# Attention with a gated MLP on one core: projections in groups of four tiles with two score blocks at their end, and another order of the first tiles and of the shift steps

## The chip, the core and the metric

The kernel runs on one core of a Trainium2 chip. The core has five engines that run side by side, each with its own queue in order: TensorE (PE, with its weight loads shown as PEld), VectorE (DVE), ScalarE (ACT), GpSimd (POOL) and SyncE (SP), which here issues all DMAs. The metric is the device time of one execution in microseconds (us).

## The reference

Layer norm feeds an attention block and an MLP; the MLP's output gates the attention's:

```
xn = layernorm(x)                               # x: 2048 x 512
q, k, v = split(xn @ wqkv)                      # 32 heads of 16
s = softmax(q @ k.T * 16**-0.5) @ v, heads joined, @ wo
h = relu(xn @ w1 + b1)**2                       # 512 -> 1792
out = x + s * silu(h @ w2 + b2)
```

All tensors are float32.

## The kernel before, in words

**Precision.** A product is made of three matmuls: both operands are split into a high and a low part (`split`, L78, on POOL, or with the high part on ACT; `split_psum`, L87, on ACT and DVE), and high x high, high x low and low x high are summed (`terms3`, L267). Softmax needs the row maximum of each score row before the exponential. Scores are therefore computed twice: once with query rows on the partitions for a maximum over 512 keys (`max_mm`, L293: one matmul of 512 columns and one DVE reduce, L313), and once with keys on the partitions for the exponential (`exp_mm`, L1270: one matmul and one ACT exponential, L1289). The maximum enters the second product as two extra rows of the query operand, a high and a low part.

**Units and blocks.** The work of attention is 32 units (4 heads by 512 queries), each of 64 maxima and of 16 blocks (128 keys): a block is four scores, four exponentials and the PV product (`pv_step`, L1293). The 512 blocks are numbered by `st`.

**Row halves.** Most matmuls contract over 64 rows, so PE takes two at a time, one in each half of its rows. The code calls the halves lanes. A lone matmul in one half leaves the other idle. A tile that is accumulated by both halves has its second half's first matmul wait for a DVE reduce that was issued behind the first half's last one.

**Start** (L1134 to L1197). `x` is loaded in 16 tiles of 128 tokens, with the four slices of V's weights between the first four. POOL splits these slices one after the other. The loop over `i` interleaves, for neighbouring tiles, statistics (`ln_stats`), normalisation (`ln_norm`), transposes by PE with ACT's copy (`ln_high`), the low part by DVE (`ln_low`), and 8 matmuls a step of projection tiles at full height (`pump`, L1111; `q_tile`, L988). There are 48 projection tiles (16 of V, 32 of Q and K) of 12 such matmuls; 16 are done here. Then the second weight load, the rings for K and Q and the loads of the first K heads and Q unit follow (L1178 to L1188). SP is not under a written order here: a scheduler places its DMAs.

**Lead** (L1202 to L1263). 31 tiles are made in row halves (`lead_halves`, L1032): 12 matmuls in the low half, then 12 in the high half, and the high half runs 23 steps late (`far`, `LAG`), beside the low half of the next tile. Each tile takes 5 maxima along. Banks rotate over three pools (`q_bank`, L980). At the end the high half's rest is flushed with one maximum for three steps. A finished tile is copied by ACT, split by POOL and stored by SP (`q_end`, L997). `b` counts tiles; loads, ring fills and stores are hung on its values.

**Main loop** (L1467). Blocks 0 and 1 carry 6 full-height matmuls each of the last tile (`slot` with `fill=6`); that tile is split into a tile of its own and its store is put off by 6 blocks (`later(6, ...)`, L1012). Blocks 2 and 3 have no extra work; from 4 on the MLP is fed in: for the first 256 tokens by `halves`, one block a slot, then by `long_slots` (L1365), four blocks each. In a long slot, two blocks run as one half with 12 dense matmuls in one lane and maxima and scores in the other. Ordinarily these take 8 maxima in two visits with a PV product behind each; here called an eight. If enough maxima are in hand (`ahead_m`, L1353, less a reserve that falls with `st`, or more freely beside a pending shift, `hosts`, L1360), they take 7 in one visit and both PV products together: a seven. The last 60 blocks carry the output projection (`wo_part`, L737), in wide slots once no maximum is left (`m_free`, L734).

**Shift** (`shift`, L336). When a unit's 64 maxima are done, `max_end` notes it (`late`), and two blocks later DVE reduces them (L338), forms the high and low part with two `scalar_tensor_tensor` steps (L340, L343), and transposes them (L347); SP stores the result (`keep`, L350) and loads it as rows of the query operand (`back`, L370). `later(n, fn)` puts a function off by n blocks, and `begin` (L1455) runs what is due.

PE's order is written out throughout; those of ACT, DVE and POOL in the start, the lead and the loop; SP's in the loop alone.

Of the kernel before, what the change touches and what calls it, by code (L numbers as in the profile page):

```python
# [16 lines left out]
P = 128  # L17
# [15 lines left out]
LAG = 8  # L33
# [3 lines left out]
EPS = 1e-5  # L37


@with_exitstack  # L40
def kernel(
# [31 lines left out]
    zero = const.tile([P, 16], F32, name="zero")  # L73
    nc.vector.memset(zero, 0.0)
# [23 lines left out]
    with ExitStack() as ph:  # L98
# [87 lines left out]
        def later(n, fn):  # L186
            waiting.append((now[0] + n, fn))
# [144 lines left out]
        def shift_due():  # L332
            if late and late[0][0] <= now[0]:
                shift(late.pop(0)[1])

        def shift(u):  # L336
            m4 = sp.tile([P, 16], F32, name="m4")
            nc.vector.tensor_reduce(m4, mxs[u], axis=AX.X, op=ALU.max)  # L338
            sh = sp.tile([P, 2, 16], F32R, name="sh")
            nc.vector.scalar_tensor_tensor(  # L340
                sh[:, 0], m4, -1.0, zero, op0=ALU.mult, op1=ALU.add
            )
            nc.vector.scalar_tensor_tensor(  # L343
                sh[:, 1], m4, -1.0, sh[:, 0].bitcast(F32), op0=ALU.mult, op1=ALU.subtract
            )
            sq = sp.tile([P, 32], F32, name="sq")
            nc.vector.transpose(sq, sh.rearrange("p i c -> p (i c)").bitcast(F32))  # L347
# [9 lines left out]
            if in_loop:  # L357
                later(1, keep)
                later(max(2, 16 * u - 9 - now[0]), back)
            else:  # L360
                keep()
                if u < 2:
                    back()
                else:
                    waiting.append((16 * u - 9, back))
# [371 lines left out]
        def wo_part():  # L737
            for k in range(15):
# [31 lines left out]
                def post():  # L770
# [9 lines left out]
                    nc.vector.tensor_tensor(g, ps[0], g, op=ALU.mult)  # L780
# [197 lines left out]
        lead = [0, 0, 0]  # L978

        def q_bank():  # L980
            lead[2] += lead[0]
            if lead[2] % 5 == 1:
                return pd.tile([P, 512], F32, name="pd_t")
            if lead[2] % 5 == 2:
                return pv.tile([P, 512], F32, name="po")
            return pe.tile([P, 512], F32, name="se")

        def q_tile(kind, m, c, last=False):  # L988
            ps = pd.tile([P, 512], F32, name="pd_t") if last else q_bank()
# [4 lines left out]
            q_end(kind, m, c, ps, last)  # L994
            yield

        def q_end(kind, m, c, ps, last=False):  # L997
            if kind == "v":
# [6 lines left out]
                return  # L1005
            if last:

                hl = pools["n"].tile([P, 2, 512], F32R, name="hl")
                raw = sp.tile([P, 512], F32, name="ot", bufs=1)
                nc.scalar.activation(raw, ps, AF.Copy)  # L1010
                split((hl[:, 0], hl[:, 1]), raw)
                later(6, lambda: qk_store(m, c, hl))  # L1012
                return
# [18 lines left out]
        def lead_halves(kind, m, c):  # L1032
            ps = q_bank()
# [3 lines left out]
            def emit(mm, lane, follow):  # L1037
# [4 lines left out]
                    start=first_ and lane == 0, stop=last_ and lane == 1,  # L1042
# [10 lines left out]
                if lane and last_:  # L1053
                    q_end(kind, m, c, ps)

            def behind(inst):
# [3 lines left out]
                [lambda mm=mm, lane=lane: emit(mm, lane, lane and mm is mms[0]) for mm in mms]  # L1060
                for lane in range(2)
            ], behind
# [81 lines left out]
        for ko in range(KO):  # L1144
            split((wa_t[:, 0, ko, 2 * P :], wa_t[:, 1, ko, 2 * P :]), raw_v[:, ko])
        for i in range(NT + 3):
            if i == 1:
# [3 lines left out]
            if 0 < i - 1 < NT:  # L1151
                ln_norm(i - 1)
            if 0 <= i - 3 < NT:
                ln_low(i - 3)
            if 0 <= i - 2 < NT:
# [10 lines left out]
            if i >= 3:  # L1166
# [5 lines left out]
                pump(8 if i > 3 else 6)  # L1172
# [8 lines left out]
        for n in range(8):  # L1181
            load_k(0, n)
# [344 lines left out]
```

## Time and profile before

| What | Value |
|---|---|
| median of 3 runs | 1639.32 us (1638.95 to 1640.37) |
| the profiled execution | 1642.99 us, span 1641.1 us |
| mean granted PE clock | 0.996 |
| PE busy | 1621.3 us (99%) |
| DVE busy | 1350.6 us (82%) |
| ACT busy | 1181.7 us (72%) |
| POOL busy | 516.4 us (31%) |
| HBM read, written | 144.84 MB, 53.99 MB |

The span runs from the first to the last instruction. Rows of the trace in order of time give start, duration, engine, source line, operation, output <- inputs, shape and count; a bracket behind them gives the idle time of the engine before it and what ended it. Rows of groups give busy time and the mean of one behind the bar. A PE row's duration holds the way through the array, so that neighbouring matmuls overlap; the distance between starts is what one costs. A table of stretches gives the length, each engine's busy time with its instructions, the granted clock (1.00 is full), the share of the DMA engines and GB/s. In the lists of waits stand the total, the number and the longest.

### The profile page before, as it was taken

How to read it: one execution, taken by the hardware profiler on the slowest of the kernel's cores; microseconds unless marked ns; L12 is line 12 of the kernel's file. 1: busy time of each engine (PE TensorE's matmuls, PEld its weight loads, DVE VectorE, ACT ScalarE, POOL GpSimd, SP SyncE). 2: the span in 40 equal slices, each digit the busy share in tenths (PEclk: the TensorE clock that was granted, in tenths of full speed). 3: DMA queues.
4: the chain of work that ended last, by engine and by line, in shares of the span. 5: the costliest groups of instructions: out<-in, count | busy, mean ns of one | idle time of the engine just before them, and what ended most of it. 6: DMA issues, size and time to landing. Idle time of an engine off the chain costs nothing.

```text
span 1641.1 us, 35386 instructions
## 1 busy us (share of the span) xinstructions
PE 1621.3 (99%) x13627; PEld 979.2 (60%) x13627; DVE 1350.6 (82%) x2335; ACT 1181.7 (72%) x2339; POOL 516.4 (31%) x541
## 2 busy tenths in 40 slices
PE   7999999999999999999999999999999999999998
PEld 6799666556656655565566556645665565454455
DVE  6399988887788888888888888888888888888843
ACT  6221477778878877787777777877877777777785
POOL 5335567513211321222123103311331133213224
PEclk9899999999999999999999999999999999999999
DMA  8596555426232522342333423343341442415444
GB/s 304 158 270 222 180 177 163 130 54 170 86 87 83 162 72 81 102 128 70 93 99 111 114 71 111 95 107 82 112 121 50 105 142 62 105 48 171 122 147 143
DMA packets 150465, 201.44 MB, mean 123 GB/s; under 512 B 50008, under 2 KB 67416, under 8 KB 148760
## 3 DMA queue, kind: packets, MB, share of 16 engines
q1 hardware_dynamic: 150296, 199.17, 41.6%
q8 instruction: 108, 1.77, 0.5%
q14 instruction: 61, 0.50, 0.1%
HBM read 144.84 MB, written 53.99 MB: 121 GB/s over the span
## 4 chain that ended last, share of the span: by engine, by line
PE 94%; DVE 2%; issue 2%; DMA 1%; POOL 0%; SPq 0%; ACT 0%; DVEq 0%
PE po L379 30%; PE pm_t L305 17%; PE pd_t L239 17%; PE se L1283 15%; PE pd_t L207 5%; PE se L1040 3%; PE pd_t L787 2%; DVE mx L313 2%; PE pd_t L1040 1%; PE po L1040 1%; PE se L991 1%; DMA ka<-k_d 1%; PE pm_t L1283 0%; DMA xt<-in_A_x_dram 0%; POOL wr_t L944 0%
## 5 line engine op out<-in xcount | busy, mean ns | idle before, releaser
L313 DVE TENSOR_REDUCE mx<-pm_t 128x1 f32<-128x512 f32 x2048 | 1267.9, 683 | 208.7 <-PE pm_t L305 123.1
L1289 ACT ACTIVATE pt<-se 128x512 f32<-128x512 f32 x1738 | 924.0, 615 | 227.3 <-PE se L1283 156.5
L305 PE MATMUL pm_t<-ka,qm 64*128 64x512 f32 x2048 | 784.5, 418 | 4.2 <-DVE mx L313 2.4
L1283 PE MATMUL se<-qe,ka 64*128 64x512 f32 x2009 | 735.0, 413 | 0.4 <-DMA qe<-sh_d 0.2
L379 PE MATMUL po<-pt,v 128*32 128x512 f32 x3554 | 526.6, 602 | 0.0
L305 PEld LDWEIGHTS pm_t<-ka,qm 64*128 64x128 f32 x2048 | 360.6, 185 | 219.5 <-DVE mx L313 205.2
L1283 PEld LDWEIGHTS se<-qe,ka 64*128 64x128 f32 x2009 | 350.5, 184 | 103.1 <-ACT pt L1289 61.8
L239 PEld LDWEIGHTS pd_t<-xc,w1s 64*128 64x128 f32 x2352 | 295.7, 187 | 47.3 <-issue 45.3
L239 PE MATMUL pd_t<-xc,w1s 64*128 64x256 f32 x2352 | 322.0, 286 | 0.0
L239 PE MATMUL pd_t<-w2t,hT 64*128 64x512 f32 x936 | 253.2, 406 | 0.0
L379 PE MATMUL po<-ex,v 128*32 128x512 f32 x542 | 226.5, 602 | 0.0
L1289 ACT ACTIVATE ex<-se 128x512 f32<-128x512 f32 x271 | 163.4, 616 | 42.1 <-PE se L1283 30.2
L239 PEld LDWEIGHTS pd_t<-w2t,hT 64*128 64x128 f32 x936 | 159.5, 184 | 48.5 <-issue 40.2
L379 PEld LDWEIGHTS po<-pt,v 128*32 128x32 f32 x3554 | 88.2, 108 | 154.3 <-issue 141.1
L558 POOL TENSOR_TENSOR r<-r 128x512 f32<-128x512 f32 x49 | 50.9, 1039 | 331.9 <-ACT r L555 331.9
L577 POOL TENSOR_TENSOR u<-u,b_t 128x512 f32<-128x512 f32 x16 | 20.7, 1296 | 365.0 <-ACT u L576 365.0
L207 PE MATMUL pd_t<-w2t,hT 64*128 64x512 f32 x408 | 106.1, 392 | 0.0
L207 PEld LDWEIGHTS pd_t<-w2t,hT 64*128 64x128 f32 x408 | 72.5, 184 | 9.6 <-DVE mx L313 0.7
L787 PE MATMUL pd_t<-wot,oc 64*128 64x512 f32 x267 | 76.9, 406 | 0.0
L417 POOL TENSOR_TENSOR ot<-ot,hl 128x512 f32<-128x512 f32 x31 | 39.8, 1284 | 109.1 <-DMA hl<-r_d 80.9
L83 POOL TENSOR_TENSOR hT<-r,hT 128x512 fp32r<-128x512 f32 x56 | 72.2, 1289 | 4.7
L1040 PE MATMUL se<-xT,wr_t 64*128 64x512 f32 x336 | 71.4, 390 | 0.0
(133 smaller groups left out, 1213.4 us busy)
## 6 DMA issues: line engine op xcount, KB each, us to landing
w1s<-w_d SPq DMA_DIRECT2D x196, 256.0 KB
k_d<-hl SPq DMA_DIRECT2D x32, 256.0 KB
xn_d<-xT SPq DMA_DIRECT2D x8, 1024.0 KB
q_d<-hl SPq DMA_DIRECT2D x16, 512.0 KB
qm<-q_d SPq DMA_DIRECT2D x128, 64.0 KB
qe<-q_d SPq DMA_DIRECT2D x128, 64.0 KB
ka<-k_d SPq DMA_DIRECT2D x32, 256.0 KB
hl<-r_d SPq DMA_DIRECT2D x31, 256.0 KB
```

Source lines behind the costliest of these rows:

```text
L83: (lo or nc.gpsimd).tensor_tensor(dst[1], raw, dst[0].bitcast(F32), op=ALU.subtract)
L207: mm = nc.tensor.matmul(out_, lh(r), rh(r), start=first_ and lane == 0, stop=last_ and lane == 1, skip_group_check=True,)
L239: mm = nc.tensor.matmul(out_, lh(r), rh(r), start=first_ and lane == 0, stop=last_ and lane == 1, skip_group_check=True,)
L305: nc.tensor.matmul(ps, qms[u][p][64 * j : 64 * j + 64, qb * P : (qb + 1) * P], kas[qd, p][64 * j : 64 * j + 64, kc * 512 : (kc + 1) * 512] ...
L313: return nc.vector.tensor_reduce(mxs[u][:, c, kc : kc + 1], ps, axis=AX.X, op=ALU.max)
L379: nc.tensor.matmul(po[32 * j : 32 * j + 32, :], vs[qd][:, (4 * kb + j) * VW : (4 * kb + j) * VW + 32], pts[j], start=(kb == 0), stop=(kb = ...
L417: nc.gpsimd.tensor_tensor(ot, ot, hl[:, 1].bitcast(F32), op=ALU.mult)
L558: nc.gpsimd.tensor_tensor(r, r, r, op=ALU.mult)
L787: inst = nc.tensor.matmul(ps[lane], oc[r, a, n, ts_], wot[r, b, n], start=m == 0 and (lane == 0 or wide), stop=m == kos and (lane == 1 or ...
L1040: inst = nc.tensor.matmul(out_, lh(r), rh(r), start=first_ and lane == 0, stop=last_ and lane == 1, skip_group_check=True,)
L1283: nc.tensor.matmul(se, kas[qd, j // 2][b : b + 64, kb * P : (kb + 1) * P], qes[u][j // 2][b : b + 64, :], start=True, stop=True,)
L1289: return nc.scalar.activation(pts[j], se, AF.Exp, scale=0.25)
```

## The change

- **Lead.** All 32 remaining tiles run in 8 groups of four (`lead_group`). Lane 0 does the first half of tiles 0 and 2 and the second half of 1 and 3; lane 1 the reverse. Both lanes begin and end a group together. `LEAD_AT` gives the places of 11 maxima in each lane (group 0 has none before its step 12). Banks are fixed: two of `pe`, one of `pd`, one of `pv`.
- **Scores.** In the last group the 8 scores and exponentials of blocks 0 and 1 are put in, after each twelfth of a lane, all of them in the third `pe` bank. The main loop begins with block 2, and the path of its own for the last tile is dropped.
- **SP** is in written order from the first K loads on; Q's pairs are loaded behind each four K loads, and some ring fills move.
- **Start.** V's slices 2 and 3 have their high parts made by ACT, and for x's first tiles the transposes come ahead of the next normalisation and statistics; the matmuls start one step earlier (3, then 9, then 8 a step) and 36 follow the loop instead of 48.
- **Shift.** Three `tensor_reduce` steps (maximum; negated maximum; negated sum of both as the low part) take the place of a reduce and two `scalar_tensor_tensor`. Store and load of the shift are run first among what is due, and before block 440 a shift may wait two blocks longer for a seven.
- **Sevens** come in couples (`seven`): one is taken only if two can be, and beside a pending shift a couple begins in the second half of a long slot.
- **Tail.** While maxima are left, an output tile is copied by ACT and multiplied by POOL instead of being multiplied by DVE; `wo_small` comes 8 blocks after its call instead of 3.

```diff
-        def later(n, fn):
-            waiting.append((now[0] + n, fn))
+        def later(n, fn, first=False):
+            waiting.insert(0 if first else len(waiting), (now[0] + n, fn))
...
-        def shift_due():
-            if late and late[0][0] <= now[0]:
+        def shift_due(slack=0):
+            if late and late[0][0] + slack <= now[0]:
...
-            m4 = sp.tile([P, 16], F32, name="m4")
-            nc.vector.tensor_reduce(m4, mxs[u], axis=AX.X, op=ALU.max)
-            sh = sp.tile([P, 2, 16], F32R, name="sh")
-            nc.vector.scalar_tensor_tensor(
-                sh[:, 0], m4, -1.0, zero, op0=ALU.mult, op1=ALU.add
-            )
-            nc.vector.scalar_tensor_tensor(
-                sh[:, 1], m4, -1.0, sh[:, 0].bitcast(F32), op0=ALU.mult, op1=ALU.subtract
-            )
+            sh = sp.tile([P, 3, 16], F32R, name="sh")
+            nc.vector.tensor_reduce(sh[:, 0].bitcast(F32), mxs[u], axis=AX.X, op=ALU.max)
+            nc.vector.tensor_reduce(sh[:, 1], mxs[u], axis=AX.X, op=ALU.max, negate=True)
...
+                nc.vector.tensor_reduce(
+                    sh[:, 2], sh[:, :2].bitcast(F32).rearrange("p i c -> p c i"),
+                    axis=AX.X, op=ALU.add, negate=True,
+                )
...
-                    nc.vector.tensor_tensor(g, ps[0], g, op=ALU.mult)
+                    else:
+                        h = ps[0]
+                        if not m_free():
+                            h = wos["f"].tile([P, D], F32, name="h", bufs=2)
+                            nc.scalar.activation(h, ps[0], AF.Copy)
+                    (nc.vector if wide or m_free() else nc.gpsimd).tensor_tensor(
+                        g, ps[0] if wide else h, g, op=ALU.mult
+                    )
...
-        for ko in range(KO):
-            split((wa_t[:, 0, ko, 2 * P :], wa_t[:, 1, ko, 2 * P :]), raw_v[:, ko])
+        for ko in range(2):
+            split_v(ko, False)
         for i in range(NT + 3):
+            if 2 <= i < 4:
+                if i == 3:
+                    split_v(3, True)
+                ln_high(i - 2)
+                ln_norm(i - 1)
+                if i == 2:
+                    split_v(2, True)
+                ln_low(i - 2)
+                rest.append(("v", i - 2, 0))
...
-        for n in range(8):
-            load_k(0, n)
-        qms[0] = load_q(0, "qm")
+        first.enter_context(tc.manual_schedule(engines={mybir.EngineType.SP}))
+        qms[0] = []
+        for p in range(2):
+            for n in range(4):
+                load_k(0, 4 * p + n)
+            load_q_pair(0, "qm", p, qms[0])
...
+        def lead_group(g):
+            items = [rest.pop(0) for _ in range(4)]
+            pools_ = [(pe, "se"), (pe, "se"), (pd, "pd_t"), (pv, "po")]
+            parts = [
+                lead_halves(*item, pool.tile([P, 512], F32, name=name), n % 2)
+                for n, (item, (pool, name)) in enumerate(zip(items, pools_))
+            ]
+            last = g == groups - 1
+            se = pe.tile([P, 512], F32, name="se") if last else None
+            streams = []
+            for lane in range(2):
+                own, other = parts[lane::2], parts[1 - lane :: 2]
+                mms = own[0][0] + own[1][0] + other[0][1] + other[1][1]
+                at = [i for i in LEAD_AT[lane] if g or i >= 12]
...
+                    if last and i % 12 == 5:
+                        kb, j = divmod(2 * (i // 12) + lane, 4)
+                        ops.append(
+                            lambda kb=kb, j=j: exp_mm(kb, j, pts.setdefault(kb, {}), False, se)
+                        )
...
+            for pair in zip(*streams):
+                for op in pair:
+                    op()
...
+        def seven(st):
+            if couple[0]:
+                couple[0] = False
+                return True
+            kept = 0 if late and st % 4 == 2 else max(0, 450 - st) // 16 * 2
+            couple[0] = ahead_m(sum(done_m) + 14 - kept, st + 4)
+            return couple[0]
```

221 lines of the change are left out of this document (98 added, 123 removed).

## The prediction

> **What bounds the kernel now.** I read the page's busy shares and its chain of waits first, then the lead stage in a table of time stretches, then the order in time of single engines where the change cuts.
>
> ```profile
> PE 1621.3 (99%) x13627; PEld 979.2 (60%) x13627; DVE 1350.6 (82%) x2335; ACT 1181.7 (72%) x2339; POOL 516.4 (31%) x541
> ```
>
> ```profile
> PE 94%; DVE 2%; issue 2%; DMA 1%; POOL 0%; SPq 0%; ACT 0%; DVEq 0%
> ```
>
> PE is the chain nearly everywhere. So an edit pays where PE runs half filled, slow or waiting, and costs where it adds PE steps. Five stretches make up the time from the lead's first half-array matmul to block 2 (124.76 us):
>
> ```profile
> 64.48:69.40 4.92, 4.00 (x17) 2.90 (x17) 1.98 (x3) 2.08 (x3) 4.17 (x3) 0.86 0.96 183
> 69.40:78.30 8.90, 8.90 (x36) 6.67 (x36) 6.35 (x10) 0.00 (x0) 0.00 (x0) 0.50 0.42 161
> 78.30:175.93 97.63, 97.50 (x837) 91.58 (x834) 90.33 (x151) 19.04 (x33) 46.64 (x51) 1.00 0.71 232
> 175.93:183.33 7.40, 7.05 (x34) 4.04 (x32) 7.40 (x13) 0.92 (x2) 3.21 (x4) 1.00 0.54 167
> 183.33:189.24 5.91, 5.57 (x24) 3.20 (x24) 4.75 (x8) 3.50 (x7) 1.91 (x2) 1.00 0.25 92
> ```
>
> Columns: stretch, length, busy PE, PEld, DVE, ACT, POOL (instructions), granted clock, DMA share, GB/s. Only the third row is full. In the first, one row half works alone (17 matmuls in 4.92 us); in the second the clock is 0.50; in the fourth only the late half's remainder is left and DVE sets the pace (7.40 of 7.40 busy); the fifth holds blocks 0 and 1 with the last tile at full height.
>
> **The sum is made against the profiled execution** (1642.99 us, span 1641.1, so 1.9 us lie around it). That is 3.67 above the median 1639.32 of the runs shown; I subtract the change from the median.
>
> **Lead in groups.** Stretches used here and below:
>
> ```profile
> 101.09:114.54 13.45, 13.45 (x119) 12.94 (x117) 12.51 (x21) 2.40 (x4) 6.19 (x7) 1.00 1.03 266
> 205.00:214.63 9.63, 9.23 (x87) 5.69 (x85) 8.81 (x16) 7.07 (x14) 6.64 (x10) 1.00 0.67 230
> 299.33:308.21 8.88, 8.88 (x68) 4.72 (x66) 8.07 (x16) 6.30 (x12) 4.65 (x5) 1.00 0.30 72
> 409.56:415.03 5.47, 5.47 (x59) 3.73 (x56) 4.28 (x8) 4.80 (x11) 1.04 (x1) 1.00 0.68 205
> 574.68:580.39 5.71, 5.71 (x59) 3.54 (x58) 4.97 (x9) 4.38 (x10) 0.91 (x1) 1.00 0.29 83
> 586.08:603.13 17.05, 17.02 (x143) 9.44 (x142) 14.31 (x27) 13.28 (x27) 2.95 (x3) 1.00 0.39 102
> 1576.05:1584.93 8.88, 8.88 (x74) 5.00 (x72) 1.38 (x2) 8.05 (x17) 2.57 (x2) 1.00 0.59 174
> ```
>
> The first row spans four lead tiles of 24 tile matmuls and 5 maxima: 116 matmuls, 58 pairs of row halves, 13.45/58 = 0.232 us a pair. After the change 32 tiles make 8 groups. A group has 96 tile matmuls and 22 maxima, 59 pairs, 13.68 us. Group 0 leaves out the maxima before step 12, and the shorter stream ends the pairing, so 96 + 16 = 56 pairs, 12.99. The last group adds 8 scores: 63 pairs, 14.61. Both halves start and end together, so rows one and four vanish. DVE keeps up: 12.51/21 = 0.596 us a maximum, 22 x 0.596 = 13.1 under 13.68, but only 0.6 is spare, so I allow 1.0 for the two shifts in the lead. The clock should stay whole, as the first maximum comes 12 steps (2.8 us) later and the K loads no longer stand on SP behind a weight load.
>
> The 8 scores all use one bank. A score's price:
>
> ```profile
> 183.36 0.47 PE L1283 MATMUL se<-qe,ka 64*128 64x512 f32 x1
> ```
>
> ```profile
> 183.01 0.60 ACT L1020 ACTIVATE raw<-pd_t 128x512 f32<-128x512 f32 x1 [3.45 <-PE pd_t L1040]
> 183.86 1.15 ACT L1289 ACTIVATE pt<-se 128x512 f32<-128x512 f32 x2 [0.25 <-DMA qm<-q_d]
> ```
>
> From the matmul's start to its exponential is 0.50, the exponential about 0.6: the bank is held 1.1 to 1.2 us. The halves' scores stand within one step of each other, so the second waits about 0.95 in PE's order, and everything behind it: 4 x 0.95 = 3.8 (bounds 1.9, if queued steps slip by, and 7.5, if all eight wait). The lead is then 12.99 + 6 x 13.68 + 1.0 + 14.61 + 3.8 = 114.5 against 124.76: **-10.3**. It does 170 maxima (before: 170, and 8 more in blocks 0 and 1).
>
> **Start.**
>
> ```profile
> 9.94 2.91 PE L991 MATMUL se<-wa_t,xT 128*128 128x512 f32 x6
> ...
> 13.35 2.12 PE L991 MATMUL se<-wa_t,xT 128*128 128x512 f32 x8
> ```
>
> Six matmuls take 2.91 where eight take 2.12: they wait for POOL, which splits V's four weight slices one after another. Now ACT makes two of the high parts and x's first transposes are copied ahead of the next normalisation. At the later rate the six cost 1.6, a gain of 1.3; **-1.3** (0, if ACT only takes the place of POOL, to -2.5, if the first tile also begins 1.2 earlier). The 16 full tiles ahead of the lead stay 16.
>
> **Hand-over to the MLP.** Before, the last tile's store was put off by 6 blocks; now the last two tiles end in the same step and SP runs in program order, so their stores stand ahead of the first w1 load.
>
> ```profile
> 183.70 0.62 POOL L82 TENSOR_SCALAR hl<-raw 128x512 fp32r<-128x512 f32 x1 [2.07 <-ACT raw L1020]
> 184.40 1.29 POOL L83 TENSOR_TENSOR hl<-raw,hl 128x512 fp32r<-128x512 f32 x1
> ...
> 192.41 0.41 POOL L82 TENSOR_SCALAR w1s<-ex 128x256 fp32r<-128x256 f32 x1 [0.40 <-DMA ex<-in_B_w_dram]
> 192.90 0.73 POOL L83 TENSOR_TENSOR w1s<-ex,w1s 128x256 fp32r<-128x256 f32 x1
> ```
>
> ```profile
> 189.34 0.39 SPq L451 DMA_DIRECT2D ex<-in_B_w_dram  x1
> ```
>
> ```profile
> 196.17 0.40 PE L207 MATMUL pd_t<-xc,w1s 64*128 64x256 f32 x2
> ```
>
> Copy 0.7, two splits of 1.95, stores 0.5: the load goes about 5.1 us after the lead's end. Load to split was 192.41 - 189.34 = 3.1, the first half's split 1.2: the MLP could begin at 9.4. Blocks 2 and 3 cover 196.17 - 189.24 = 6.9. PE waits 2.5, and 0.5 more for the second half: **+3.0** (0, if the loads aren't held, to 4.5, if POOL is a split behind).
>
> **Sevens.** A pair of blocks in a long slot does 8 maxima (5.71 in the fifth row above) or, with enough in hand, 7 (5.47 in the fourth). One is in hand for each maximum beyond 96 + 4 per block and the reserve; block 2 is now met with 170 instead of 178, so 8 sevens become eights: 8 x 0.22 = **+1.7** (1.5 to 2.0). The coupling moves some pairs of sevens. The sixth row holds an eight and an isolated couple that began in a first half: 17.05 - 5.71 = 11.34, where two sevens in a run take 10.94. By the planner's rule about four couples in the MLP's first product begin in a second half now: up to 4 x 0.4 gained, none if the entry costs there too; **-0.8** (+0.8 to -1.6). `first=True` and the later `wo_small` change the order of DMAs with blocks to spare: 0.
>
> **Shift steps.**
>
> ```profile
> L340 DVE SCALAR_TENSOR_TENSOR sh<-m,zero 128x16 fp32r<-128x16 f32 x30 | 7.7, 258 | 1.0
> ```
>
> ```profile
> L338 DVE TENSOR_REDUCE m<-mx 128x16 f32<-128x64 f32 x30 | 6.3, 210 | 0.0
> ```
>
> ```profile
> 207.65 0.96 DVE L340 SCALAR_TENSOR_TENSOR sh<-m,zero 128x16 fp32r<-128x16 f32 x1
> ```
>
> ```profile
> 1107.17 1.15 DVE L343 SCALAR_TENSOR_TENSOR sh<-m,sh 128x16 fp32r<-128x16 f32 x1
> ```
>
> ```profile
> 207.54 1.04 POOL L516 TENSOR_TENSOR r<-r 128x512 f32<-128x512 f32 x1 [3.12 <-ACT r L513]
> ```
>
> The two-input step at 207.65 started inside POOL's operation and ended with it (208.61 and 208.58). The one-input reduce has a mean of 210 ns over its 30, so it isn't held. The three blocks around the held step took 9.63 (second of the seven stretches), around one that ran freely 8.88 (third): 0.75 lost. DVE's order in time shows three such places outside a couple, the first and the last being the two rows above; in a couple the 16 PV matmuls hide them. The new steps, a negated reduce and a reduce over two rows of 16, each read one tensor; I price them as the 210 ns row and give back 0.8 a place: **-2.5** (0, if they are held as well, to -2.6; below that nothing, since no other place lies on PE's path). The Trainium skill's "VectorE: DVE Perf Modes", Rules for kernel authors, calls `tensor_reduce` on a hot path the slowest DVE operation and advises restructuring; taken at its word this term would be 0 or above and the sum -7.1. The row of 210 ns against 258 with waits speaks against it here.
>
> **Tail.** With 8 maxima left at block 486 the new test no longer refuses a seven; one maximum stays over, so the slot at 488 isn't run wide. It needs 2 x (14 x 0.232 + 1.9) = 10.3 instead of 8.88 (seventh row), the 1.9 from
>
> ```profile
> 412.61 1.92 PE L379 MATMUL po<-pt,v 128*32 128x512 f32 x16
> ```
>
> That is +1.4; the seven gives back 0.2, and two products of 0.68 leave DVE's queue of maxima,
>
> ```profile
> 1556.72 0.68 DVE L780 TENSOR_TENSOR g<-pd_t,g 128x512 f32<-128x512 f32 x1
> ```
>
> worth 0.6: **+0.6** (-0.8 to 1.4).
>
> Sum: -10.3 - 1.3 + 3.0 + 1.7 - 0.8 - 2.5 + 0.6 = -9.6; 1639.3 - 9.6 = **1629.7 us** (the profiled execution 1633.4).
>
> **Rivals.**
> *Covered hand-over and cheap bank*: the loads pass in time and half the bank waits are filled: -9.6 - 3.0 - 1.9 = -14.5, 1624.8. For it: POOL's first w1 split (192.41) stood 3.8 us ahead of the first MLP matmul (196.17), so there is cover that I may undercount. Against it: SP cannot pass a store that waits.
> *Clock falls at the hand-over*: the stretch with clock 0.50 followed pauses of under 2 us with half the array idle, and blocks 2 and 3 are thin too. Another such 8.90 us at half speed costs 4.45: -5.1, 1634.2. By the Trainium skill's "TensorE: Matmul & The Clock Gate", Part 1, the clock falls after an idle window of about 3.4 us, which this 3.0 us wait would not fill; by that rule the forecast stands.
> *DVE paces the groups*: the page's mean for a maximum is longer,
>
> ```profile
> L313 DVE TENSOR_REDUCE mx<-pm_t 128x1 f32<-128x512 f32 x2048 | 1267.9, 683 | 208.7 <-PE pm_t L305 123.1
> ```
>
> and 22 x 0.683 = 15.03, 1.35 over a group; six groups cost 8.1: -1.5, 1637.8. Against it: back to back DVE took 0.596.
> *Slower, SP in program order*: waits of SP in the stretch 40 to 190 us, longest first,
>
> ```profile
> SPq L964 <- POOL hl L83: 14.7, 7, 3.2
> SPq L1003 <- ACT vt L1000: 14.6, 4, 11.8
> SPq L967 <- POOL hl L83: 6.7, 8, 1.0
> SPq L967 <- POOL hl L82: 4.8, 5, 1.5
> SPq L370 <- DMA sh_d<-sq: 4.4, 2, 2.3
> ```
>
> are 45.2 us; if they all line up ahead of a unit's Q loads, which have 48 maxima (2.2 groups, 30 us) of slack, the maxima stop for 15 us and PE behind them: +5.4, 1644.7. It turns slower from a lateness of 13 us on.
>
> **Numbers.** About 0.2% (3.3 us) is what a measurement of this kernel can tell from no change: 1636.0 to 1642.6. Chances: forecast 0.56, covered 0.18, clock 0.11, DVE pace 0.10, SP 0.05. The first three are faster: 0.85; the fourth the same, 0.10; the last slower, 0.05. The range 1623.5 to 1637.0 takes in the first three with their terms' bounds and leaves out most of the other two.
>
> **What would show it.** The stretch from the first half-array matmul to block 2 should be about 114 us with clock 1.00 throughout; groups of 22 maxima 13.7 apart; four PE pauses of about 1 us in the last group; SP's w1 load about 5 us after the last tile and PE waiting 2 to 4 us before the MLP's first matmul; no shift step over 0.25 us; 66 runs of seven maxima before block 440, where DVE's order in time shows 74 today. It is wrong if groups take over 14.5, if the clock dips, or if the main loop from block 60 on is over 3 us longer.

## The result and the profile after

| | before | after |
|---|---|---|
| median of 4 runs each | 1639.84 us (1638.95 to 1640.44) | 1648.68 us (1646.99 to 1652.24) |
| the profiled execution | 1642.99, span 1641.1 | 1649.66, span 1647.8 |

The change makes the kernel slower, by half a per cent: ratio 1.0051, 95% interval 1.0037 to 1.0066. The forecast was 1629.7. In the page of after PE is busy 4.5 us less than before, yet the chain of waits is no longer PE alone:

```profile
PE 1616.8 (98%) x13639; PEld 966.1 (59%) x13639; DVE 1344.2 (82%) x2331; ACT 1183.9 (72%) x2343; POOL 515.7 (31%) x540
...
PE 91%; issue 2%; DMA 2%; POOL 1%; DVE 1%; SPq 1%; ACT 1%; DVEq 0%; POOLq 0%; ACTq 0%
```

So work was saved and time was lost to waits (half clock costs PE about 4.5 us in the trace of before and 5.4 in that of after). Where, is seen by five marks that both traces have: the first half-array matmul, the begin of block 2, the reciprocal at the end of the first unit and that at the end of the 30th, and the end of the span.

| stretch | before | after | difference | forecast |
|---|---|---|---|---|
| up to the first half-array matmul | 64.48 | 65.50 | +1.0 | -1.3 |
| lead, up to block 2 | 124.76 | 123.75 | -1.0 | -10.3 |
| block 2 to the first unit's end (hand-over) | 59.54 | 65.80 | +6.3 | +2.2 |
| to the 30th unit's end (loop) | 1312.12 | 1309.59 | -2.5 | -0.8 |
| to the end (tail) | 80.20 | 83.16 | +3.0 | +0.6 |

In the column of the forecast the shift steps' three places stand where the prediction has them, one in the hand-over and two in the loop. The rows of the marks, from DVE's order in time, before and after:

```profile
248.78 0.24 DVE L403 RECIPROCAL sm<-sm 128x16 f32<-128x16 f32 x1
...
1560.90 0.24 DVE L403 RECIPROCAL sm<-sm 128x16 f32<-128x16 f32 x1
```

```profile
255.05 0.24 DVE L403 RECIPROCAL sm<-sm 128x16 f32<-128x16 f32 x1
...
1564.64 0.24 DVE L403 RECIPROCAL sm<-sm 128x16 f32<-128x16 f32 x1
```

The lead of after in a table of stretches, cut at the begin of groups 0, 1, 5, 6 and 7, at block 2 and where the blocks run evenly again:

```profile
65.50:78.55 13.05, 13.05 (x113) 11.86 (x114) 9.33 (x15) 3.18 (x5) 6.82 (x4) 1.00 1.01 288
78.55:134.11 55.56, 55.56 (x474) 47.37 (x472) 54.64 (x92) 10.66 (x20) 23.53 (x27) 1.00 0.86 280
134.11:156.83 22.72, 16.06 (x122) 12.71 (x118) 14.02 (x23) 2.28 (x4) 9.50 (x11) 0.85 0.67 232
156.83:170.94 14.11, 14.11 (x121) 10.86 (x118) 13.97 (x26) 2.50 (x5) 7.83 (x9) 1.00 0.42 155
170.94:189.25 18.31, 16.22 (x129) 12.59 (x126) 14.14 (x24) 7.01 (x13) 8.40 (x9) 1.00 0.41 138
189.25:209.12 19.87, 14.89 (x92) 7.38 (x92) 11.53 (x18) 10.17 (x19) 11.44 (x19) 0.83 0.76 235
```

Group 0 takes 13.05, four full groups 55.56 (13.9 each), the last one 18.31. One group takes 22.72 and has PE busy for 16.06 of it. Without this stop of 8.8 us the lead would take 114.9, close to the forecast of 114.5. Inside the stop:

```profile
137.96:144.56 6.60, 0.00 (x0) 0.00 (x1) 1.03 (x2) 0.60 (x1) 2.48 (x4) 0.81 0.96 331
144.56:148.95 4.39, 4.39 (x20) 3.50 (x22) 1.50 (x3) 0.00 (x0) 3.15 (x3) 0.51 0.84 318
```

PE stands still for 6.60 us, and the next 20 matmuls run at a clock of 0.51; half of their 4.39 us, 2.2, makes up the rest of the 8.8. The list of waits from 134 to 150 us names the chain, to be read from PE upward, and SP's order in time shows what stood ahead of the stores:

```profile
ACT raw L1011 <- POOL hl L84: 11.4, 3, 7.9
DVE mx L314 <- PE pm_t L306: 8.5, 3, 7.3
POOL hl L83 <- DMA k_d<-hl: 7.1, 2, 6.5
PEld pd_t L1030 <- ACT raw L1011: 7.1, 1, 7.1
PE pd_t L1030 <- ACT raw L1011: 6.7, 1, 6.7
```

```profile
127.23 0.65 SPq L350 DMA_DIRECT2D sh_d<-sq  x1
132.54 2.08 SPq L370 DMA_DIRECT2D qe<-sh_d  x4
134.66 0.39 SPq L136 DMA_DIRECT2D ka<-k_d  x1
135.10 0.57 SPq L1271 DMA_DIRECT2D xn_d<-xT  x1
135.77 2.41 SPq L974 DMA_DIRECT2D k_d<-hl  x2
138.28 1.04 SPq L971 DMA_DIRECT2D q_d<-hl  x1
```

PE waits for a bank that ACT has not copied, ACT for a raw buffer, POOL for one of three split buffers (`hlp`), and that for a store. The store was issued at 135.8, behind SP's wait of 4.7 us (127.88 to 132.54) for the shift's own store. At the hand-over `xc` is loaded behind the stores of the last two tiles:

```profile
189.95 0.56 SPq L451 DMA_DIRECT2D ex<-in_B_w_dram  x1
190.61 1.49 SPq L974 DMA_DIRECT2D k_d<-hl  x2
193.73 0.53 SPq L971 DMA_DIRECT2D q_d<-hl  x1
194.31 2.65 SPq L493 DMA_DIRECT2D xc<-xn_d  x4
```

PE waits for it, and then half the clock is gone:

```profile
PE pd_t L208 <- DMA xc<-xn_d: 4.1, 2, 2.9
```

```profile
195.80:198.74 2.94, 0.00 (x0) 0.03 (x1) 0.69 (x1) 0.60 (x1) 0.74 (x2) 1.00 0.95 273
200.53:206.98 6.45, 6.45 (x33) 4.06 (x35) 2.39 (x4) 2.51 (x5) 3.46 (x7) 0.50 0.74 220
```

### The profile page after: what moved, and what is told of

Read it like the earlier page. It is cut to its first block, busy times and chain, and to the rows that moved or that the text cites. A ratio compares the mean times of both kernels' runs of the same rounds, so it can differ in the third digit from the quotient of the medians.

```text
span 1647.8 us, 35386 instructions
## 1 busy us (share of the span) xinstructions
PE 1616.8 (98%) x13639; PEld 966.1 (59%) x13639; DVE 1344.2 (82%) x2331; ACT 1183.9 (72%) x2343; POOL 515.7 (31%) x540
## 4 chain that ended last, share of the span: by engine, by line
PE 91%; issue 2%; DMA 2%; POOL 1%; DVE 1%; SPq 1%; ACT 1%; DVEq 0%; POOLq 0%; ACTq 0%
PE po L379 29%; PE pd_t L240 16%; PE pm_t L306 16%; PE se L1224 15%; PE pd_t L208 6%; PE se L990 2%; PE se L1030 2%; PE pd_t L794 1%; PE po L1030 1%; PE pd_t L1030 1%; DVE mx L314 1%; DMA sh_d<-sq 0%; PE pm_t L1086 0%; DMA hl<-r_d 0%; DMA xc<-xn_d 0%
## 5 line engine op out<-in xcount | busy, mean ns | idle before, releaser
L306 PE MATMUL pm_t<-ka,qm 64*128 64x512 f32 x2048 | 795.9, 417 | 0.9 <-DVE mx L314 0.6
L555 ACT ACTIVATE r<-pd_t,b_t 128x256 f32<-128x256 f32 x98 | 42.1, 496 | 32.7 <-PE pd_t L240 32.7
```

Source lines behind the costliest of these rows:

```text
L306: nc.tensor.matmul(ps, qms[u][p][64 * j : 64 * j + 64, qb * P : (qb + 1) * P], kas[qd, p][64 * j : 64 * j + 64, kc * 512 : (kc + 1) * 512] ...
L555: nc.scalar.activation(r[:, i], ps[:, i * CW : (i + 1) * CW], AF.Relu, bias=b1_t[:, fo : fo + 1])
```

## The experiments

All traces are compared with that of the changed kernel by the same marks. The table has one profiled execution of each (time, then the five stretches, in us):

| run | time | start | lead | hand-over | loop | tail |
|---|---|---|---|---|---|---|
| before | 1642.99 | 64.48 | 124.76 | 59.54 | 1312.12 | 80.20 |
| after | 1649.66 | 65.50 | 123.75 | 65.80 | 1309.59 | 83.16 |
| e1 | 1649.58 | 65.06 | 123.16 | 64.41 | 1309.56 | 85.61 |
| e2 | 1643.63 | 65.86 | 114.88 | 65.22 | 1309.64 | 86.20 |
| e3 | 1646.27 | 68.44 | 118.79 | 65.57 | 1309.43 | 82.17 |
| e4 | 1641.65 | 65.04 | 116.64 | 65.31 | 1309.44 | 83.37 |
| e5 | 1648.66 | 64.97 | 124.28 | 65.51 | 1309.62 | 82.52 |
| e6 | 1646.49 | 66.32 | 124.42 | 64.75 | 1309.38 | 79.83 |
| e7 | 1648.86 | 64.63 | 124.56 | 64.77 | 1309.93 | 83.11 |
| e8 | 1642.39 | 65.17 | 115.54 | 64.86 | 1309.52 | 85.51 |
| e9 | 1635.74 | 65.91 | 114.87 | 63.98 | 1309.47 | 79.77 |
| e10 | 1635.90 | 65.11 | 114.90 | 63.47 | 1310.91 | 79.71 |
| e11 | 1630.18 | 65.49 | 111.66 | 62.02 | 1309.54 | 79.69 |
| e12 | 1634.61 | 64.29 | 120.07 | 58.67 | 1309.52 | 80.25 |
| e13 | 1635.65 | 64.24 | 120.86 | 58.67 | 1309.85 | 80.28 |
| e14 | 1643.95 | 65.69 | 123.96 | 60.21 | 1309.57 | 82.77 |
| e15 | 1655.39 | 65.23 | 123.93 | 66.22 | 1315.01 | 83.21 |
| e16 | 1634.56 | 65.19 | 111.67 | 66.61 | 1309.53 | 79.70 |

Single executions differ, those of the kernel before by up to 8 us (below). The loop differs least: it takes 1309.4 to 1309.9 in the 13 kernels here that have the changed loop as it is or without its last seven.

**The stop: order, buffers or full DMA engines.** Four edits, one each:

```diff
 # e1_rows_later
-                    back()
+                    later(4, back)
 # e2_ring_five
-        hlp = right(qs, "hlp", 3)
+        hlp = right(qs, "hlp", 5)
 # e3_bias_early: the loads of b1_t and b2_t from k == 4 to ahead of
 # the first load_k
 # e4_sp_free
-        first.enter_context(tc.manual_schedule(engines={mybir.EngineType.SP}))
```

> The changed kernel, but in the lead the load of a unit's shift rows is issued four tiles after the store that it must wait for, instead of right behind it. In the changed kernel the seventh group of the lead takes 22.7 us where the others take 13.7 to 14.1: a stop of 8.8 us. Theory A, SP's written order: SP waits 4.6 us for the shift's store to land and issues the rows for 2.1 us, and the finished tiles' stores stand behind it, so the buffer of POOL's split comes free late. Then the stores at 135.8 go some 6.5 us earlier, the stop falls below 2 us, the clock stays whole there, and the time falls by 7 to 9 us to about 1640. Theory B, three buffers for two tiles that end together are too few: the stop stays over 4 us. Theory C, the DMA engines are full (busy share 1.0 from 110 to 120 us) and the stores land late whatever their order: the stop changes by less than 1.5 us.

> The changed kernel with five buffers instead of three for the split tiles of the lead. Two more buffers are half a group, 7 us, of slack for the stores. Theories A and B both let the stop of 8.8 us fall below 2 us (A: the stores are as late as before, 6.5 us, but nobody waits for them; B: no tile waits for a buffer any more); the time falls by 7 to 9 us. Theory C, full DMA engines: the lateness only moves to a later group, and the lead becomes shorter by less than 3 us.

> The changed kernel with the loads of the two bias vectors taken out of the lead (SP spends 3.5 and 2.7 us on issuing them at 115 us) and put ahead of the first loads of K. If SP's lateness is a sum (theory A in its wide form), 6.2 us less of it lets the stop of 8.8 us fall below 3 us. If only the shift's round trip counts (A in its narrow form) or the buffers alone (B), the stop stays over 6 us, because SP has caught up by 123 us in either case. Theory C, full DMA engines: 256 KB less in the full stretch, under 1 us. At the new place the loads may hold the first loads of K and cost up to 3 us ahead of the lead.

> The changed kernel with SP not under a written order in the lead: the scheduler places its DMAs, as in the kernel before. Theory A: the scheduler puts finished tiles' stores ahead of the wait for the shift, the stop falls by 5 us or more. Theory B: the stop stays over 4 us. At the hand-over the loads of the MLP's first data may also pass the last tiles' stores: of the 6.3 us that stretch cost, up to 3 us come back if so.

The group of the stop, in the four kernels in this order:

```profile
133.66:155.75 22.09, 16.36 (x120) 12.65 (x118) 14.01 (x22) 2.88 (x5) 11.95 (x14) 0.85 0.66 237
```

```profile
134.47:148.29 13.82, 13.82 (x121) 11.07 (x118) 13.66 (x22) 2.29 (x4) 7.57 (x9) 1.00 0.92 324
```

```profile
137.04:154.75 17.71, 15.67 (x120) 12.28 (x118) 13.98 (x22) 2.28 (x4) 8.26 (x10) 0.90 0.70 247
```

```profile
135.40:149.22 13.82, 13.82 (x120) 11.06 (x118) 13.66 (x22) 2.29 (x4) 7.58 (x9) 1.00 0.49 180
```

With the rows later the stop stays (22.09): the shift's round trip alone, my first theory, is refuted. In that kernel the stores were issued at 125.7 to 128.1, and POOL got its buffer only at 133.8. The DMA view from 120 to 130 us shows what the engines did meanwhile:

```profile
DMA  9999997799943310469699479997996988999999
GB/s 203 255 220 238 261 319 167 110 82 62 65 27 12 7 1 1 57 188 172 197 139 270 57 107 262 221 320 172 164 188 131 311 287 303 344 393 418 418 401 442
DMA packets 4234, 2.00 MB, mean 200 GB/s; under 512 B 3652, under 2 KB 3652, under 8 KB 4184
...
b_t<-in_B_b_dram SPq DMA_DIRECT2D x1, 7.0 KB
```

One load of 7 KB, `b1`, reads 1792 elements of 4 bytes that lie apart. The rate falls to 62 GB/s while the engines are 0.9 busy, and then with their share to 1 GB/s; the stores come behind what has queued up. The Trainium skill's "DMA: Bandwidth & Descriptors", Rules for kernel authors, says that a last dimension that isn't contiguous becomes one descriptor for each element; the 3652 packets under 512 B, about two for each element, agree. With the bias loads moved, the group falls to 17.71, though not to 13.8, and the lead begins 2.9 us later, at 68.44, behind the moved loads. Five buffers or SP's free order remove the stop wholly (1643.63 and 1641.65 in one run each). So there were two delays ahead of the stores. Taking both away, with three buffers left:

```diff
 # e8_rows_and_bias: e1, and
-                    nc.sync.dma_start(b2_t, b2[None, :].to_broadcast([P, D]))
...
+            if b == 24:
...
+                nc.sync.dma_start(b2_t, b2[None, :].to_broadcast([P, D]))
```

> The changed kernel with three buffers as it stands, but with both suspected causes of the stop taken away: the shift's rows are loaded four tiles after their store, and the two bias loads (one of them 7 KB in packets of 4 bytes) go to tile 24, past the full stretch. Taken alone, the rows left 8.2 us of the stop of 8.8 and the bias loads 3.8. Theory, a queue in order (SP's and the DMA engines') with three buffers as its slack: with both gone the stop falls below 1 us and the seventh group takes 13.7 to 14.5. Theory, three buffers are too few whatever the order: at least 3 us stay. At tile 24 the bias loads may make a stop of their own: then the eighth group is over 20 us instead of 18.3.

```profile
133.78:148.26 14.48, 14.08 (x120) 11.05 (x118) 13.95 (x22) 2.28 (x4) 8.25 (x10) 1.00 0.67 233
```

The stop is 0.6 us, and the last group took 18.32, so the bias loads at tile 24 hurt nobody. Shown: two things stand ahead of the stores, SP's wait and the bias loads. Each alone makes a stop (3.8 us with SP's wait left in e3, 8.2 with the bias loads left in e1), together 8.8, so both have to go; the slack is the number of split buffers, and five of them mend it as well. Not shown: which part of the bias loads does it, the small packets, the 256 KB of `b2` or the 6.4 us that SP spends on issuing both in e1; e3 and e8 move all of it together. The totals of e2 and e8 fall by less than the stop, because their tails are 3.0 and 2.4 us longer, at a clock of 0.91 from 1580 to 1600 us (1.00 in the changed kernel); e1's is too. What makes it fall there is open. SP's free order (e4) gives back only 0.5 at the hand-over, where up to 3 were thought possible.

**The hand-over.** The last two tiles' stores wait in the list of what is put off, in buffers of their own; for one of them two exponential tiles are borrowed:

```diff
+                if (m, c) == (3, 3):
+                    two = [free_pt.pop(), free_pt.pop()]
...
+                    waiting.append((6, store))
...
+                if (m, c) == (7, 3):
...
+                    waiting.append((7, lambda: qk_store(m, c, hl)))
 # e5_store_later gives the two tiles back in store, e14 at block 16:
+                    waiting.append((16, lambda: free_pt.extend(two)))
```

> The changed kernel, but the stores of the last two tiles of the lead are put off to blocks 6 and 7, as the kernel before did with its last tile; their split halves stand in buffers of their own. Theory, stores ahead of the MLP's loads: in the changed kernel PE waits 2.9 and 1.2 us for xc at 196 to 200 us and runs blocks 2 to 5 in part at a clock of 0.66. With xc issued at about 189.5 instead of 194.3, these waits fall below 1 us in sum, the clock stays whole, and 3 to 5 us of the 6.3 come back. Rival, POOL's queue: the four splits of the last tiles (7.8 us) end at 193.7 in either case and the split of w1 stands behind them; then less than 1.5 us come back and PE waits for w1 instead of xc.

> The changed kernel with the last two tiles' stores put off, with the borrowed buffers given back at block 16 instead of block 6. In the first try the fifth PV product of the main loop came 5.8 us earlier than in the changed kernel, before an exponential waited 3.35 us for a borrowed buffer. Theory, the hand-over is worth those 5.8 us: at the first unit's end 5 to 6.5 us less than the changed kernel, the clock whole from 190 to 220 us, the stop at 138 us unchanged. Rival, another wait at block 6 follows whatever the buffers: below 2 us.

The first try took the wait for `xc` away (0.5 us left) and gave it back at once: an exponential waited for the store of the tile that I had lent, and the clock fell behind it. The row of ACT in e5:

```profile
209.01 2.21 ACT L1246 ACTIVATE pt<-se 128x512 f32<-128x512 f32 x4 [3.35 <-DMA q_d<-pt]
```

With the tiles kept until block 16, PE is busy for 18.27 of the 20.00 us behind block 2 in e14, at full clock, and the first unit ends at 249.86 instead of 255.05, 5.2 us less, as expected; the stop of the lead was there as before (22.91).

```profile
190.00:210.00 20.00, 18.27 (x150) 9.75 (x151) 16.16 (x27) 14.21 (x29) 13.17 (x21) 1.00 0.81 257
```

**The tail.**

```diff
 # e6_no_late_seven
-            couple[0] = ahead_m(sum(done_m) + 14 - kept, st + 4)
+            couple[0] = st < 480 and ahead_m(sum(done_m) + 14 - kept, st + 4)
```

> The changed kernel without sevens from block 480 on; so no maximum stays over at block 488. Theory: the maximum left over costs twice, a thin slot in place of a wide one (10.9 instead of 8.9 us) and the last unit's shift about 10 us later, whose rows PE then waits for (1.2 us). Expected from block 480 on: PE's wait for the rows gone, one slot wide again, 2.5 to 3.5 us less; the output products moved to ACT and POOL keep a gain of up to 0.6 over the kernel before. Rival, the products on ACT and POOL cost the tail: less than 1 us comes back.

In after one maximum stays over, and with it the last unit's shift:

```profile
1578.22 0.69 DVE L314 TENSOR_REDUCE mx<-pm_t 128x1 f32<-128x512 f32 x1 [6.61 <-PE pm_t L306]
```

```profile
1593.30 0.47 PE L1224 MATMUL se<-qe,ka 64*128 64x512 f32 x1 [1.23 <-DMA qe<-sh_d]
```

In e6 the last three maxima run at 1571.10 and the shift at 1573.0 instead of 1581.8. From the end of the 30th unit to the end after needs 83.16, e6 79.83, before 80.20:

```profile
1564.64:1647.80 83.16, 76.01 (x564) 43.38 (x560) 26.18 (x48) 55.62 (x111) 29.29 (x24) 0.98 0.42 140
```

```profile
1564.87:1644.70 79.83, 73.93 (x564) 42.28 (x560) 26.96 (x49) 55.53 (x111) 30.64 (x25) 0.99 0.45 146
```

**The start.** e7 puts the start of the kernel before (the loop over `i` and V's slices) into the changed kernel.

> The changed kernel with the start of the kernel before (V's slices all on POOL, normalisation ahead of the transposes, 8 matmuls a step from the fourth step on, 48 behind the loop). Theory: in the changed start PE is a step ahead of the low part of x that DVE makes, and waits 2.4 us for it at 28 us behind a split that stands ahead on DVE; the gain of 1.1 us up to the second tile is lost there. So the first half-array matmul comes at 64.3 to 65.0 instead of 65.5. Rival, the later DMAs of the start (SP's stores, the rings) set the lead's begin: it stays at 65.5 or becomes later. Either way the stop at 138 us keeps its size, 7 to 10 us.

In after PE waits in the start for the low part of x:

```profile
30.88 1.90 PE L990 MATMUL se<-xT,wa_t 128*128 128x512 f32 x7 [2.42 <-DVE xT L1094]
```

In e7 this wait is 0.53, and the lead begins at 64.63. But the same start gives 64.97 to 66.32 in the other kernels here that share it, and 65.49 and 65.19 in e11 and e16 with the start of before. The wait is shown, the net loss of about 1 us is not settled.

**The shift steps.** e12 and e13 are one kernel: before with the three reduces alone. e15 is the changed kernel with the steps of before.

```diff
 # e12, e13: into before; e15: the same taken out of the changed kernel
-            nc.vector.scalar_tensor_tensor(
-                sh[:, 0], m4, -1.0, zero, op0=ALU.mult, op1=ALU.add
-            )
...
+            nc.vector.tensor_reduce(sh[:, 1], mxs[u], axis=AX.X, op=ALU.max, negate=True)
```

> The kernel before with the shift's three reduces alone. Theory, the two-input step is held by POOL: three places of 0.8 us each are gained, near 207, 1107 and 1570 us; no shift step is over 0.25 us; 1.6 to 2.6 us less than before. Rival, the held steps are covered: below 0.8.

> The kernel before with the three reduces alone, timed. Its trace gained 3.6 us at shift steps (four places) and 4.7 us in the lead, where the profiled execution of the kernel before had a stretch at half clock that this one lacks. Theory, that stretch belongs to single executions and not to the kernel: the median falls by the 3 to 4 us of the shift steps, to 1635.5 to 1637. Rival, the reduces bring the clock back as well: the median falls by 7 to 9 us, to 1631 to 1633.

> The changed kernel with the shift steps of the kernel before (a reduce and two steps with two inputs). Theory, the reduces save 0.8 to 0.9 us at each place where POOL works beside an uncovered shift: 2 to 4 us more than the changed kernel from block 2 on, in steps of 0.7 to 1.0, with held steps of 0.5 to 1.2 us on DVE. Rival, in the changed kernel's order the shifts fall beside other work: under 1 us.

Against the trace of before, e12 gains 0.87 ahead of the first unit's end, 0.90 between the first two, 0.95 at the 19th to 20th and 0.48 near the 29th, where e13 gains only 0.10; it is 3.4 in all (3.1 in e13), and no step took over 0.22. The expected places near 207 and 1107 us paid; the one near 1570 paid nothing (tail 80.20 before, 80.25 in e12), and the held step at 254.79 paid in its stead. Taking the reduces out of the changed kernel (e15) costs 5.8 us of span, 5.4 of it in the loop, more than the 2 to 4 expected; there 15 of the 60 two-input steps behind block 2 are over 0.25, where in before 6 are. Each of these 21 began inside an operation of POOL and ended at most 0.05 us after it. The mean of the first step nearly doubles (258 before):

```profile
L343 DVE SCALAR_TENSOR_TENSOR sh<-m,zero 128x16 fp32r<-128x16 f32 x32 | 15.3, 479 | 1.1
```

But e12's trace is 8.3 us shorter than that of before, not 3.4. The rest is in one place, the stretch that the prediction quotes with a clock of 0.50 and 36 matmuls. The same 8.90 us in e12:

```profile
69.40:78.30 8.90, 8.59 (x67) 6.97 (x68) 8.61 (x15) 0.60 (x1) 0.00 (x0) 1.00 0.45 164
```

Nearly twice the matmuls at full clock, with nothing changed there. Block 2 begins in e12 at

```profile
184.36 0.50 PE L1282 MATMUL se<-qe,ka 64*128 64x512 f32 x1
```

where before it began at 189.24. Timed, the reduces bring 1635.5 against 1640.42 (8 and 11 runs, ratio 0.9977, interval 0.9966 to 0.9988), a few us and not eight. And the kernel before in the timed series of e11 and e13 had mean clocks of 0.999 or 1.000 in 19 of 22 executions (1638.05 to 1642.45 us) and 0.996 or 0.997 in three (1643.56, 1646.04, 1646.43); the profiled one, at 0.996 and 1642.99, is of the second kind. So the clock's fall belonged to that execution and not to the median. One execution of e13's eight fell too (1641.31, clock 0.996).

**All mended.**

```diff
 # e9_all_mended: e1, e2, bias loads at tile 24, e14, e6
 # e10_sevens_before: e9 with ahead_m, hosts and shift_due() of before
 # e11_scores_two_pools: e9, the start of before, and
-    exp_mm(kb, j, pts.setdefault(kb, {}), False, se)
+    exp_mm(kb, j, pts.setdefault(kb, {}), lane == 1, None if lane else se)
 # e16_xc_first: e11 and
-            load_w1(0)
-            load_xc(0)
+            load_xc(0)
+            load_w1(0)
```

> The changed kernel with five split buffers, the shift's rows four tiles behind their store, the bias loads at tile 24, the last two tiles' stores behind the MLP's loads (their borrowed buffers are given back ten blocks later than in the first try, where an exponential waited for one) and no seven from block 480 on. Theory, the lost 17 us lie in these places and add up: stop 8.5, hand-over 5 to 6, tail 3, together 16 to 18 below the changed kernel: 1630 to 1633. Rival, the waits are one queue's and the next one takes over (a later tile's store, the loads of w1): over 1637.

> The mended kernel with the rule for sevens of the kernel before (one at a time, beside a pending shift at once, no wait of a shift for a seven). It also refuses the late seven. Theory, the sum's terms: couples gain 0.8 and the eight maxima fewer in hand cost 1.7 under either rule, so this version is 0.4 to 1.5 slower than the mended one between blocks 60 and 480. Rival, the couples cost: the trace of the changed kernel loses 1.9 us between 475 and 570 us where before none was lost; then this version is 1 to 3 us faster there.

> The mended kernel with the start of the kernel before, and the upper lane's scores of blocks 0 and 1 in a bank of the maxima's pool instead of the lower lane's bank. Theory, the bank makes the second score wait: the four PE pauses of the last group (0.85 each) go, the group takes 15.0 instead of 18.3 us, and with the start 0.8 more: 3 to 4.5 us below the mended kernel, 1626 to 1629. Rival, the maxima need that bank: each score there holds a maximum's bank for 1.1 us, DVE waits instead, and less than 1 us is won in the group.

> The version with two pools for the scores, and xc loaded ahead of the first w1 slice, because PE still waits 2.1 us for xc there while w1's split stands behind POOL's last tiles. Theory: 0.5 to 1.0 us of that wait go, the median is 1629.5 to 1631. Rival, w1 comes later by as much: no change within 0.3 us in the trace.

e9 took 1635.74 in one run, above its 1630 to 1633. The stop (8.9) and the tail (3.4) came back whole, the hand-over only by 1.8: PE's waits for `xc` were 0.95 at most, and the clock fell all the same:

```profile
187.30:194.00 6.70, 5.12 (x28) 2.22 (x26) 2.76 (x4) 2.39 (x4) 3.65 (x8) 0.76 0.96 288
194.00:197.00 3.00, 3.00 (x23) 2.78 (x20) 1.98 (x3) 1.49 (x3) 2.83 (x6) 0.50 0.54 171
```

e10 is 1.4 us slower than e9 from the first to the 30th unit's end (1310.91 against 1309.47, from the same marks), so the new rule for sevens, with the shift's wait for one, is worth that in this kernel; the rival, that couples cost, falls. In e11 the last group takes 15.09 instead of 18.31, as expected, without a pause for the bank:

```profile
162.06:177.15 15.09, 15.09 (x129) 12.19 (x126) 14.27 (x24) 6.40 (x12) 7.50 (x9) 1.00 0.44 152
```

It runs at 1630.99 (6 runs) against 1640.74: ratio 0.9938, interval 0.9921 to 0.9954, the fastest version here, though above the 1626 to 1629 that I expected. e16 is slower than e11 by its trace, 4.3 us at the first unit's end; timed it is 1634.18, ratio 0.9965, interval 0.9952 to 0.9978. PE no longer waits for `xc` but for w1's split, longer than before, so neither theory held:

```profile
PE pd_t L208 <- POOL w1s L83: 5.1, 1, 5.1
```

## Why the prediction was wrong, step by step

By the table of stretches the trace of after is 16.3 us longer than forecast: the start by 2.3, the lead by 9.3, the hand-over by 4.1, the tail by 2.4, while the loop is 1.8 shorter. Against the median it is 19.0, since the profiled execution of before lay 3.67 above the median that was subtracted from and that of after only 0.98 above its own. The largest step that failed is the one that put SP's written order at nothing.

**The subtraction from the median.** The sum took the lead of the profiled execution, 124.76, and the difference from the median. But 124.76 held a stretch at half clock that most executions lack: with it gone, the lead of the kernel before takes 120.1 (e12, 64.29 to 184.36) or 120.9 (e13, 64.24 to 185.10). The lead's -10.3 should have been about -5.6 by e12's, and the whole forecast 1634.4. The prediction had seen the sign, that the profiled execution lay 3.67 above the median, and the clock of 0.50; it did not put the two together.

**The lead's groups** were right: 13.05, then 13.9 on average against 13.68, the allowance of 1.0 for shifts being short by 0.5; the last group 18.31 against 18.41, with four pauses in place as foretold. e11 confirms the cause of the pauses. DVE was busy 54.64 of 55.56 in the four full groups; whether a little of the rival "DVE paces the groups" is in the 13.9, no run separates.

**SP in program order**, the rival on the slower side at 0.05, came true by another door. The prediction asked whose loads stand behind SP's waits and found 30 us of slack. It did not ask the same of the stores: the stop, 8.8, is in no term of the sum. Two tiles now end in one step, the ring has three buffers, and the next user of a buffer is half a group, 7 us, away. It also held SP's waits for the only delay, where the bias loads were the second (e1 and e3 against e8).

**The hand-over** (+3.0) failed in size: two waits of 2.94 and 1.20, and then 6.45 us at a clock of 0.50, which costs 3.2 more. The stores ahead of the loads are shown as the cause (e14). But the load that went 5.1 us after the lead's end was `xc`'s (194.31), which the prediction did not look at; w1's, which it priced, went at 189.95, ahead of the last stores. The prediction had the clock's fall as a rival of its own and let a rule talk it down: the table of the Trainium skill's "TensorE: Matmul & The Clock Gate", Part 1, puts the fall behind an idle window of about 3.4 us. Here it fell behind two pauses of 2.94 and 1.20 with a thin stretch between, and in e9 behind pauses of 0.95 and less; in e11, with 2.1 us of such pauses, it did not fall. The measurement decides: thin stretches were enough, and not each time.

**The start** (-1.3) was +1.0 in this trace. The gain up to the second tile came, but PE then ran one step ahead of the low parts that DVE makes, and waited 2.42 behind a split on DVE's queue. The step costed what was removed and not what PE met next.

**Shift steps** (-2.5) were right for the kernel before: of the prediction's three places two are the rows that it quotes, and between them DVE's order has one held step outside the lead, at 254.79; the stretches of the three gain 0.87, 0.90 and 0.95 in e12, 2.7 in sum. The held steps at 1389.65 and 1570 us gave nothing, as it said. But the places were counted in the kernel before: in the changed kernel the reduces are worth 5.8, since its order puts more shifts beside POOL's work (15 held steps against 6). Here the Trainium skill's "VectorE: DVE Perf Modes", Rules for kernel authors, which calls `tensor_reduce` the slowest operation, would have misled: three reduces never took over 0.22.

**Sevens and couples** (+1.7 and -0.8) held in kind. DVE's order in time shows 74 rows of exactly seven maxima before block 440 in the kernel before and 66 in after, as foretold. The loop takes 1309.52 in the kernel before with the reduces alone (e12), 1310.91 with the changed order, eight sevens fewer and the old rule (e10), and 1309.47 with the new rule (e9). So the order with its eight sevens fewer costs 1.4, and the new rule gives 1.4 back; the two cancel, and the loop's gain of 2.5 is that of the reduces alone (2.6 in e12, 2.3 in e13). That all of the first 1.4 is the sevens' is argued, not shown, and the parts do not simply add: without the reduces the changed loop is 5.4 longer (e15).

**The tail** (+0.6) had the maximum left over and the thin slot, +1.4, in it. It missed what hangs on that maximum: the last unit's shift, 9 us later, whose rows PE then waited for. Without the late seven the tail is 0.4 shorter than before (e6), and the reduces alone leave it as it was (e12), so the moved products and the later `wo_small` gave at most that, as far as one trace tells.

## What to carry to other kernels

Before subtracting a gain from a median, see whether the profiled execution has anything, such as a stretch at half clock, that the median may not have. When a queue is put in written order, list for each entry who waits behind it on both sides: loads and the buffers that stores set free. Where two producers are made to finish together, count the buffers for the burst and not for the mean, and ask of a maximum, a store or a shift that is left over what hangs on it.

## What the hardware showed that I had not expected

- While a load of 7 KB in elements of 4 bytes was under way, the rate of all DMAs fell to 62 GB/s at a busy share of 0.9 and then to 1 GB/s (e1, 121 to 124 us); the stores issued next, from 125.7, set their buffer free at 133.84.
- The clock fell to 0.50 behind pauses of under 1 us in a thin stretch (e9), stayed whole behind similar ones (e11), and differed between executions of one kernel (the stretch at 69 to 78 us).
- A two-input step of DVE with 128x16 elements that began inside an operation of POOL lasted until that operation's end, up to 1.22 us (e15); otherwise it took 0.17 to 0.22, and a reduce over four times the input at most 0.22.
